# Where expert weights may land during the attention, and when the leftover pairs get their low part

## The chip, the core and the metric

The program runs on one NeuronCore of a Trainium2 chip. Its engines are PE (TensorE, matmuls; PEld is its weight load), DVE (VectorE), ACT (ScalarE), POOL (GpSimd) and SP (SyncE), which here issues nearly all DMA transfers. The metric is the device time of one execution in microseconds, as the median of several runs. Every DMA that SP issues goes into one queue, served by the core's 16 DMA engines.

## What is computed

Three layers follow one another, all in fp32 (as two fp32r parts, high and low, where PE takes fp32r):

```python
# attention, 8 batches x 8 heads x 576 positions x 64: decayed linear scores, no softmax
scores = q @ k.T / 8
ret = (scores * gamma[h] ** (i - j) * (i >= j)) @ v          # x: 4608 x 512
# soft mixture of 8 experts with 4 slots each
logits = x @ phi
slot_input = softmax(logits, axis=tokens).T @ x              # 32 x 512
slot_out[e] = relu(slot_input[e] @ w1[e]) @ w2[e]            # w1: 512x1024, w2: 1024x512
y = softmax(logits, axis=slots) @ slot_out                   # 4608 x 512
# bilinear layer
h = (y @ m1) * (y @ m2) @ w3
out = h @ w_out
```

y has only 32 rows of freedom per token, so the kernel never forms (y @ m1) * (y @ m2) per token. It forms products of pairs of slots once (ph, pl), multiplies them with W = w3 @ w_out into a matrix G, and multiplies each token's pairs of slot weights with G.

## The kernel before, in words

**Attention, 0 to about 160 us.** A loop over 36 units of 128 positions (`for u in range(NU)`, L758 on). Each unit issues, among others, the products of masked scores with v (`emit_pv`), the state update of the next unit (`emit_state(u + 1)`), the scores of unit u+2 (`emit_qk`), transposes (`emit_turns`) and the products with the state (`emit_inter`). Beside it the weights of the bilinear layer come in as 40 "pieces" of 512 KB (`load_piece`), each converted from 64-bit words by ACT, DVE and POOL (`conv_list`, one piece per unit, its last step on DVE is L497). A piece goes into one of four raw buffers and so waits until the piece four before it is converted. Pieces 30 to 39 are converted in the experts' stage.

**What sets the order of loads.** SP issues its list in order, and each transfer waits on SP until its target is free. Inside the loop loads are not written where they are decided: `later` puts a function into the list `waiting`, and `pace(behind)`, called at three points of each unit (behind `emit_pv`, behind `emit_qk`, and at the unit's end), takes one function from it and makes the loads that it issues wait for the PE instruction `behind`. A function may turn out to issue nothing: `load_k` past the last pair of blocks (it then only puts its buffer into `free`), or `load_expert` with no free place. In the last six units three `load_expert` are listed per unit.

**Places.** A place is a tile of 128 x 1024 fp32, 512 KB. qb (3), vb (3), rb (2) and kb (3) hold q, v, raw k and scaled k; kt_place holds turned k for the scores; p_places, s_place and xt_places hold masked scores, states and outputs. An expert's weights are eight loads of 512 KB, four for the first layer and four for the second, 64 in all; each takes the first tile in `free` (`load_expert`, L577 on). Places of q, v and raw k go into `free` in the loop after their last use; those of kb, kt_place, p_places and s_place behind the loop (L834).

**Experts' stage, about 169 to 250 us.** For each expert `emit_l1` (L600) and `emit_l2` (L620), between them the matmuls of W (`emit_Ws`, L564) and conversion steps. The four tiles of a layer go back into `free` as soon as it is issued, and further expert loads wait for them.

**G, about 256 to 290 us.** `pairs(cb)` forms the products of slot pairs of block cb on DVE (L1033 to L1035) and their high parts on ACT (L1036); `pairs_low(cb)` the low parts on DVE (L1040). `pleft` and `pleft2` are the leftover pairs, formed on POOL (L1053, L1056); L1061 (ACT) and L1062 (POOL) form their high and low part `phl`. `tick()` runs the eviction of the last W block (L572 on ACT, L573 on DVE). PE does twelve matmuls for each of eight blocks (`g_mm`, L1048), and behind block 0 sixteen for the leftover pairs (L1078), which read `phl` and all eight blocks of W. `pair_prep` (L642 to L649) prepares the tokens' pairs for the output stage on POOL and ACT during G.

**Output stage, about 290 to 400 us.** Nine tiles of 512 tokens, 52 matmuls each (L1114, L1123 to L1125), evicted and stored.

Of the kernel before, what the change touches and what calls it, by code (L numbers as in the profile page):

```python
# [16 lines left out]
ALU = mybir.AluOpType  # L17
# [4 lines left out]
NU = NTOK // 128  # L22
# [9 lines left out]
def retention_softmoe_bilinear(  # L32
# [257 lines left out]
    def emit_state(u):  # L290
        if tail(u):
            return
        x, c = units[u][1], block_of(u)
        for p in range(4):
            for h, a in halves:
                nc.tensor.matmul(  # L296
                    out=sbank[a, x, p], lhsT=k_tile(u)[:, x, p, h], rhs=v_tile(u)[:, 1 - h, x, p],
                    start=(c == 0 and x == 0 and p == 0), stop=True, skip_group_check=True,
                )
        if x == 1:  # L300
            Sn = sb[(c + 1) % 2]
            if c < 3:
                nc.scalar.copy(out=Sn, in_=sbank)
            else:
                for p in range(4):
                    nc.scalar.activation(out=Sn[:, :, p], in_=sbank[:, :, p], func=ACTF.Copy, scale=stab_sb[:, 8, p:p + 1])
# [105 lines left out]
    def after(i, j):  # L412
        tc.add_manual_dep(i.ins, j.ins.name, mybir.DependencyInfo(mybir.DependencyClass.Sync, mybir.DependencyReason.DATA), reason="pace")
# [173 lines left out]
    waiting = []  # L587

    def pace(behind):
        if waiting and behind is not None:  # L590
            for i in waiting.pop(0)():
                after(i, behind)

    hr_of, ht_of = {}, {}

# [57 lines left out]
    with tc.manual_schedule():  # L653
# [94 lines left out]
        for u in range(NU):  # L748
            T, r = divmod(u - 4, 4)

            def next_load():
                if nl[0] < min(len(pieces), done[0] + NRAW):
                    came.append(max(at[0], 2))
                    nl[0] += 1
                    return [load_piece(nl[0] - 1)]
                return load_expert()

            at[0], ended = u, None  # L758
            def next_k():
                if first_of_pair(u + 4):  # L760
                    scale_k(u + 4)
                    later(lambda n=pairs_in_order.index(units[u + 4][0]) + RBUF: load_k(n))

            if u > 0:
                next_k()
            run(subs)
            run_copies()
            run(adds)
            next_conv(u - 2)
            run_conv(1)  # L770
            if u == 2:
                emit_kt(5)
                misc[:] = [bank[2]]
            if u >= 6 and r == 2:
                emit_exp(T)
            done_pv = emit_pv(u)
            if u == 0:
                emit_kt(2)
            emit_xt(u)
            pace(done_pv)  # L780
            if u + 1 < NU:
                emit_state(u + 1)
            if u == 0:
                emit_kt(3)
                next_k()
                output_factors(2)
                output_factors(3)
            if u + 2 < NU:
                done_qk = emit_qk(u + 2)
                pace(done_qk)  # L790
                emit_p(u + 2)
            if u >= 8 and r == 0:
                emit_z(T - 1)
                emit_slots(T - 1)
            if u >= 2:
                ended = emit_turns(u - 4, u + 4)
            if u + 1 < NU:
                ended = emit_inter(u + 1) or ended
            if u == 1:
                emit_kt(4)  # L800
            if last_of_item(u):
                k = units[u][0]
                if k + VBUF < len(items):
                    later(lambda k=k: load_v(k + VBUF))
                else:
                    free.append(vb[k % VBUF])
            if u + 1 < NU and last_of_item(u + 1):
                k = units[u + 1][0]
                if k + QBUF < len(items):
                    later(lambda k=k: load_q(k + QBUF))  # L810
                else:
                    free.append(qb[k % QBUF])
            if u >= 7 and r == 3:
                emit_dT(T)
            run_conv(1)
            if u != 1:
                for _ in range(2 if u in TWICE else 1):
                    later(next_load)
            if u >= NU - 6:
                for _ in range(3):  # L820
                    later(load_expert)
            if u >= 2:
                pace(ended)
            if u >= 5 and r == 1:
                emit_logits(T)
            run_conv(4)
# [4 lines left out]
        run(subs)  # L831
        run_copies()
        run(adds)
        free.extend([*kb, *p_places, s_place, kt_place])  # L834
        load_expert(4)
        load_pieces()
        close_pool("psum")
# [218 lines left out]
        nc.gpsimd.tensor_tensor(out=twice, in0=half(0), in1=half(16), op=ALU.add)  # L1056
        pairs(0)
        pairs_low(0)
        tick()
        pairs(1)  # L1060
        nc.scalar.copy(out=phl[:, :, 0], in_=pleft2)  # L1061
        nc.gpsimd.tensor_tensor(out=phl[:, :, 1], in0=pleft2, in1=phl[:, :, 0], op=ALU.subtract)  # L1062
        which = [tmp.tile([32, 1], F32, tag=t, name=t) for t in ("beta", "negm")]
        for i in range(2):
            nc.vector.tensor_reduce(out=which[i], in_=ident[0:32, 16 * i:16 * i + 16], axis=AX.X, op=ALU.add)
# [141 lines left out]
```

## Time and profile before

| | |
|---|---|
| median of 3 runs | 400.6 us (399.61 to 401.44) |
| the profiled execution | 402.09 us |
| its span, first to last instruction | 400.3 us |
| PE busy | 378.1 us, 94% of the span |
| DVE, ACT, POOL busy | 254.7, 198.8, 172.7 us |
| moved by DMA | 108.75 MB, mean 272 GB/s |
| mean granted TensorE clock | 0.991 of full speed |

The span is cut into stages as above. The share of busy time is a mean over stages with different limits; within a stage one asks which wait ends last. PE's matmuls overlap, and their ends are modelled, so a busy PE need not be at its peak: start-to-start distances tell the rate. A granted clock of 1.00 is 2.4 GHz, one of 0.50 is 1.2 GHz.

### The profile page before, as it was taken

The numbers are of one execution on the slowest core, as the hardware profiler recorded it, in microseconds if no ns is written. First come the engines' busy times: TensorE is split into PE (matmuls) and PEld (weight loads), VectorE is DVE, ScalarE is ACT, GpSimd is POOL, SyncE is SP. The second block draws the span as 40 slices with busy tenths as digits, with TensorE's granted clock in tenths as the row PEclk, the third lists the DMA queues.
The fourth block names the chain that finished last, engine by engine and source line by source line (L and its number), as shares of the span: only waits on it lengthen the run. The fifth ranks groups of instructions, "written<-read, shape, count | busy, mean of one in ns | idle before, by whom it ended". The sixth has DMA issues, their size and how long they took to land.

```text
span 400.3 us, 10956 instructions
## 1 busy us (share of the span) xinstructions
PE 378.1 (94%) x4447; PEld 283.7 (71%) x4447; DVE 254.7 (64%) x432; ACT 198.8 (50%) x424; POOL 172.7 (43%) x158
## 2 busy tenths in 40 slices
PE   6989998989999998999999899979999999999995
PEld 4878787868978877655655444738787777787774
DVE  3648998998889996527775541468576353455400
ACT  2336686887778765235535321315434444443432
POOL 2633765666554464016544330116724335543420
PEclk9999999999999999999999999969999999999999
DMA  7899999999989987999999999690168989998643
GB/s 241 299 335 352 318 349 305 274 373 366 286 266 349 301 278 283 326 407 409 406 411 408 409 408 319 140 193 1 49 137 179 235 199 243 236 217 215 158 94 94
DMA packets 48211, 108.75 MB, mean 272 GB/s; under 512 B 7584, under 2 KB 10016, under 8 KB 48160
## 3 DMA queue, kind: packets, MB, share of 16 engines
q1 hardware_dynamic: 47008, 107.85, 84.0%
q8 instruction: 35, 0.57, 0.6%
q10 hardware_dynamic: 1152, 0.20, 0.3%
q14 instruction: 16, 0.13, 0.1%
HBM read 97.41 MB, written 10.62 MB: 270 GB/s over the span
## 4 chain that ended last, share of the span: by engine, by line
PE 70%; DMA 15%; DVE 8%; issue 3%; ACT 1%; POOL 1%; ACTq 0%; SPq 0%; POOLq 0%
PE bank L1123 9%; PE bank L1125 8%; PE bank L1124 8%; PE bank L564 7%; PE output L282 5%; PE scores L253 5%; DMA k<-in_ew 5%; PE bank L1048 5%; PE output L316 4%; DMA q<-in_ew 3%; DMA kt<-in_ew 3%; PE state L296 2%; PE bank L600 2%; PE bank L620 2%; DMA q<-in_q 2%
## 5 line engine op out<-in xcount | busy, mean ns | idle before, releaser
L644 POOL TENSOR_TENSOR cc<-mw_sb,cc 128x512 fp32r<-128x512 f32 x36 | 46.0, 1299 | 57.0 <-ACT cc L643 55.7
L564 PE MATMUL bank<-wop,w3p 128*128 128x512 f32 x192 | 50.8, 406 | 0.0
L523 POOL TENSOR_TENSOR vals<-vals,msb 128x512 int32<-128x512 int32 x24 | 30.9, 1288 | 41.4 <-DVE vals L497 34.6
L263 DVE TENSOR_TENSOR pm<-scores,msb 128x1024 f32<-128x1024 f32 x31 | 37.8, 1219 | 11.4 <-PE scores L253 11.1
L564 PEld LDWEIGHTS bank<-wop,w3p 128*128 128x128 f32 x192 | 34.1, 188 | 15.0 <-issue 8.7
L643 ACT CAST cc<-mw_sb 128x512 fp32r<-128x512 f32 x36 | 22.2, 616 | 44.0 <-DVE mw_sb L642 34.7
L1123 PE MATMUL bank<-w3p,cc 128*128 128x512 f32 x108 | 43.1, 399 | 0.0
L1125 PE MATMUL bank<-w3p,cc 128*128 128x512 f32 x108 | 42.1, 390 | 0.0
L1124 PE MATMUL bank<-w3p,cc 128*128 128x512 f32 x108 | 42.0, 389 | 0.0
L282 PE MATMUL output<-pm,v 128*64 128x128 f32 x512 | 35.6, 279 | 2.3 <-issue 1.8
L533 POOL TENSOR_TENSOR w3p<-vals,w3p 128x512 fp32r<-128x512 f32 x16 | 21.1, 1317 | 37.3 <-ACT w3p L528 33.9
L642 DVE TENSOR_TENSOR mw_sb<-lga,raw 128x512 f32<-128x512 f32 x32 | 29.2, 954 | 12.3 <-POOL cc L644 12.0
L253 PE MATMUL scores<-q,kt 64*128 64x128 f32 x496 | 36.0, 285 | 0.0
L523 POOL TENSOR_TENSOR mw_sb<-mw_sb,msb 128x512 int32<-128x512 int32 x16 | 20.5, 1281 | 30.6 <-DVE mw_sb L497 23.0
L1127 ACT ACTIVATE mw_sb<-bank,rz 128x512 f32<-128x512 f32 x36 | 24.7, 686 | 17.6 <-PE bank L1125 9.4
L282 PEld LDWEIGHTS output<-pm,v 128*64 128x64 f32 x512 | 27.5, 136 | 7.6 <-issue 5.9
L253 PEld LDWEIGHTS scores<-q,kt 64*128 64x128 f32 x496 | 30.1, 187 | 2.6 <-issue 0.8
L192 POOL TENSOR_TENSOR k<-kr,msb 128x512 f32<-128x512 f32 (+1 forms) x30 | 26.1, 890 | 5.4 <-DMA kr<-in_v 5.4
L504 ACT ACTIVATE msb<-raw 128x512 int32<-128x512 uint32 x40 | 27.8, 696 | 0.0
L220 ACT COPY kt<-pair 128x512 f32<-128x512 f32 x26 | 15.3, 587 | 25.0 <-PE pair L219 24.9
L1123 PEld LDWEIGHTS bank<-w3p,cc 128*128 128x128 f32 x108 | 20.3, 188 | 7.1 <-issue 2.9
L1125 PEld LDWEIGHTS bank<-w3p,cc 128*128 128x128 f32 x108 | 20.3, 188 | 4.4
(226 smaller groups left out, 767.2 us busy)
## 6 DMA issues: line engine op xcount, KB each, us to landing
q<-in_q SPq DMA_DIRECT2D x20, 512.0 KB, 6.2
raw<-expt SPq DMA_DIRECT2D x36, 256.0 KB, 4.5
kr<-in_v SPq DMA_DIRECT2D x16, 512.0 KB, 5.8
v<-in_v SPq DMA_DIRECT2D x16, 512.0 KB, 6.5
raw<-in_m SPq DMA_DIRECT2D x16, 512.0 KB, 6.1
raw<-in_w SPq DMA_DIRECT2D x16, 512.0 KB, 6.4
out_x<-mw_sb SPq DMA_DIRECT2D x64, 128.0 KB, 2.5
k<-in_ew SPq DMA_DIRECT2D x14, 512.0 KB, 10.2
```

What stands on the lines that cost most here:

```text
L192: (nc.vector if first else nc.gpsimd).tensor_tensor(out=Ks[:, :, 0:m, h], in0=K[:, 1 - h, :, 0:m], in1=ktab(c, h)[:, 0:m].unsqueeze(1).uns ...
L253: last = nc.tensor.matmul(out=ps[:, p], lhsT=ktb[u % 2][a, p], rhs=Q[a, :, x, p], start=True, stop=True)
L263: nc.vector.tensor_tensor(out=p_places[u % 2].rearrange("p (g t) -> p g t", g=8), in0=(pair if u == 1 else scores).rearrange("p (g t) -> p ...
L282: last = nc.tensor.matmul(out=xt_view(p)[side(p, h)], lhsT=v_tile(u)[:, 1 - h, x, p], rhs=p_main(u)[:, h, p], start=(block_of(u) == 0 and ...
L504: lambda: nc.scalar.activation(out=p.bitcast(I32), in_=lo, func=ACTF.Copy, scale=2.0 ** -29),
L523: nc.gpsimd.tensor_tensor(out=ti, in0=ti, in1=parts[i % 2].bitcast(I32), op=ALU.add)
L564: nc.tensor.matmul(out=ps, lhsT=x, rhs=y, start=(k8 == 0 and part == 0), stop=(k8 == 7 and part == 2))
L642: eng.tensor_tensor(out=e, in0=x, in1=y[:, m], op=ALU.mult)
L644: nc.gpsimd.tensor_tensor(out=cl[m], in0=e, in1=ch[m], op=ALU.subtract)
L1123: nc.tensor.matmul(out=ob, lhsT=ch[m][:, sl], rhs=gh[m], start=False, stop=False)
L1124: nc.tensor.matmul(out=ob, lhsT=ch[m][:, sl], rhs=gl[m], start=False, stop=False)
L1125: nc.tensor.matmul(out=ob, lhsT=cl[m][:, sl], rhs=gh[m], start=False, stop=(m == 3))
```

## The change

Four edits. `pace` takes functions from the list until one issues loads, so that a listed load without a place uses no pace point. The three places of scaled k go into `free` right behind the `emit_state` that reads them last, and kt_place behind the last `emit_qk` that reads it; in return they are no longer freed behind the loop. Three `load_expert` per unit are listed in the last nine units instead of six. And in G the two instructions for `phl` stand ahead of `tick()` and `pairs(1)`.

```diff
--- before.py
+++ after.py
@@ -587,9 +587,11 @@
     waiting = []
 
     def pace(behind):
-        if waiting and behind is not None:
-            for i in waiting.pop(0)():
-                after(i, behind)
+        loads = []
+        while waiting and not loads and behind is not None:
+            loads = waiting.pop(0)()
+        for i in loads:
+            after(i, behind)
 
     hr_of, ht_of = {}, {}
 
@@ -780,6 +782,9 @@
             pace(done_pv)
             if u + 1 < NU:
                 emit_state(u + 1)
+                n = pairs_in_order.index(units[u + 1][0]) if units[u + 1][1] else 0
+                if n + KBUF >= len(pairs_in_order):
+                    free.append(kb[n % KBUF])
             if u == 0:
                 emit_kt(3)
                 next_k()
@@ -789,6 +794,8 @@
                 done_qk = emit_qk(u + 2)
                 pace(done_qk)
                 emit_p(u + 2)
+                if u + 2 == NU - 2:
+                    free.append(kt_place)
             if u >= 8 and r == 0:
                 emit_z(T - 1)
                 emit_slots(T - 1)
@@ -816,7 +823,7 @@
             if u != 1:
                 for _ in range(2 if u in TWICE else 1):
                     later(next_load)
-            if u >= NU - 6:
+            if u >= NU - 9:
                 for _ in range(3):
                     later(load_expert)
             if u >= 2:
@@ -831,7 +838,7 @@
         run(subs)
         run_copies()
         run(adds)
-        free.extend([*kb, *p_places, s_place, kt_place])
+        free.extend([*p_places, s_place])
         load_expert(4)
         load_pieces()
         close_pool("psum")
@@ -1056,10 +1063,10 @@
         nc.gpsimd.tensor_tensor(out=twice, in0=half(0), in1=half(16), op=ALU.add)
         pairs(0)
         pairs_low(0)
+        nc.scalar.copy(out=phl[:, :, 0], in_=pleft2)
+        nc.gpsimd.tensor_tensor(out=phl[:, :, 1], in0=pleft2, in1=phl[:, :, 0], op=ALU.subtract)
         tick()
         pairs(1)
-        nc.scalar.copy(out=phl[:, :, 0], in_=pleft2)
-        nc.gpsimd.tensor_tensor(out=phl[:, :, 1], in0=pleft2, in1=phl[:, :, 0], op=ALU.subtract)
         which = [tmp.tile([32, 1], F32, tag=t, name=t) for t in ("beta", "negm")]
         for i in range(2):
             nc.vector.tensor_reduce(out=which[i], in_=ident[0:32, 16 * i:16 * i + 16], axis=AX.X, op=ALU.add)
```

Lines behind the edits shift: L600 becomes L602, L620 L622, L1036 L1043, L1048 L1055, L1061 L1066, L1062 L1067, L1078 L1085.

How the order moves, first on SP in units 28 to 33 of the attention, before; `raw` is a piece, a load from `in_ew` an expert load, the number behind a name tells tiles of one kind apart (kr_104 and kr_105 are raw k, k_106 to k_108 scaled k).

```order
L183 DMA v_101<-in_v 128x2x512
L479 DMA raw<-in_w 128x512
L176 DMA q_99<-in_q 128x1024
L479 DMA raw<-in_w 128x512
L184 DMA v_102<-in_v 64x512 x2
L479 DMA raw<-in_w 128x512
L583 DMA kr_104<-in_ew 128x1024
L583 DMA kr_105<-in_ew 128x1024
L583 DMA q_100<-in_ew 128x1024
L479 DMA raw<-in_w 128x512
L583 DMA v_103<-in_ew 128x1024
L479 DMA raw<-in_w 128x512
```

All expert loads of the loop but the very first (ew0) stand behind the last load of v (L184).

The same stretch of SP's list after the change.

```order
L583 DMA kr_104<-in_ew 128x1024
L183 DMA v_101<-in_v 128x2x512
L479 DMA raw<-in_w 128x512
L583 DMA k_107<-in_ew 128x1024
L176 DMA q_99<-in_q 128x1024
L479 DMA raw<-in_w 128x512
L583 DMA kr_105<-in_ew 128x1024
L184 DMA v_102<-in_v 64x512 x2
L479 DMA raw<-in_w 128x512
L583 DMA k_108<-in_ew 128x1024
L583 DMA q_100<-in_ew 128x1024
L479 DMA raw<-in_w 128x512
```

Three expert loads now stand among the last loads of v and q, the second of them in a place of scaled k; the pieces and loads of q and v keep their order.

SP's list from there to the first load into a place of masked scores (pm_94), which is behind the loop, before.

```order
L583 DMA q_98<-in_ew 128x1024
L583 DMA v_101<-in_ew 128x1024
L583 DMA q_99<-in_ew 128x1024
L479 DMA raw<-in_w 128x512
L583 DMA v_102<-in_ew 128x1024
L583 DMA k_106<-in_ew 128x1024
L583 DMA k_107<-in_ew 128x1024
L583 DMA k_108<-in_ew 128x1024
L583 DMA pm_94<-in_ew 128x1024
```

The three places of scaled k are loaded last of these, behind the loop.

The same after the change.

```order
L583 DMA kt<-in_ew 128x1024
L583 DMA v_103<-in_ew 128x1024
L583 DMA k_106<-in_ew 128x1024
L583 DMA q_98<-in_ew 128x1024
L479 DMA raw<-in_w 128x512
L583 DMA v_101<-in_ew 128x1024
L583 DMA q_99<-in_ew 128x1024
L583 DMA v_102<-in_ew 128x1024
L479 DMA raw<-in_w 128x512
L583 DMA pm_94<-in_ew 128x1024
```

From the first to pm_94 there are 12 expert loads now, where there were 11, and the four into k places and kt stand inside the loop; up to v_102, the last place freed in the loop, 12 are issued instead of 8 (one more, ew0, much earlier in both).

ACT at the start of G, before; the copies into `wop` are the high parts of pairs, L572 is the eviction of the last W block, the load into `gs` is L1061.

```order
L1036 CAST wop<-mw_sb 128x128 x2
L1036 CAST wop<-mw_sb 128x256
L572 CAST w_3532<-bank_2622 128x512
L1036 CAST wop<-bank_2622 128x512
L1061 CAST gs<-mw_sb 128x8x32
L1036 CAST wop<-bank_2627 128x512
L1085 COPY acc<-bank_2626 32x512
L1036 CAST wop<-bank_2622 128x512
L647 CAST cs<-mw_sb 128x512
```

L1061 stands behind the eviction and behind the high part of block 1.

ACT at the start of G after the change.

```order
L1043 CAST wop<-mw_sb 128x128 x2
L1043 CAST wop<-mw_sb 128x256
L1066 CAST gs<-mw_sb 128x8x32
L572 CAST w_3534<-bank_2625 128x512
L1043 CAST wop<-bank_2625 128x512
L1043 CAST wop<-bank_2630 128x512
L1092 COPY acc<-bank_2629 32x512
L1043 CAST wop<-bank_2625 128x512
L649 CAST cs<-mw_sb 128x512
```

The copy into `gs` has moved up by two rows, ahead of the eviction; POOL's row for L1062 keeps its place between L1056 and the tokens' first pairs.

## Rows read from the trace of the kernel before

**Rows 1.** The page: busy time by engine; shares of the chain that ended last.

```profile
PE 378.1 (94%) x4447; PEld 283.7 (71%) x4447; DVE 254.7 (64%) x432; ACT 198.8 (50%) x424; POOL 172.7 (43%) x158
...
PE 70%; DMA 15%; DVE 8%; issue 3%; ACT 1%; POOL 1%; ACTq 0%; SPq 0%; POOLq 0%
```

**Rows 2.** Windows: length, busy us (count) by engine, clock, DMA share, GB/s.

```profile
136.00:160.00 24.00, 22.61 (x528) 18.70 (x528) 19.85 (x34) 16.11 (x38) 11.63 (x10) 1.00 0.82 275
175.00:240.00 65.00, 61.80 (x459) 34.54 (x458) 38.59 (x90) 27.43 (x60) 28.87 (x22) 1.00 1.03 409
200.00:250.00 50.00, 45.95 (x332) 24.29 (x322) 24.84 (x57) 16.44 (x37) 16.75 (x13) 1.00 1.02 392
264.00:270.00 6.00, 6.00 (x14) 3.18 (x15) 3.24 (x6) 0.59 (x1) 1.20 (x1) 0.50 1.01 191
```

**Rows 3.** Chain of waits, 236 to 292 us: start, length, what held it.

```profile
239.26 8.99 DMA k<-in_ew
...
264.00 6.64 PE bank L1078 x16
270.63 19.06 PE bank L1048 x84
```

**Rows 4.** Timeline of PE, experts 1 and 5: start, length, line, operation.

```profile
179.43 0.64 PE L600 MATMUL bank<-v,slotm 128*32 128x256 f32 x8
...
181.30 3.06 PE L564 MATMUL bank<-wop,w3p 128*128 128x512 f32 x12
...
219.14 1.07 PE L600 MATMUL bank<-k,slotm 128*32 128x256 f32 x16
...
223.36 2.34 PE L564 MATMUL bank<-wop,w3p 128*128 128x512 f32 x9
```

**Rows 5.** Timelines of SP and DVE; then single issues at 153.9, 156.4, 178.4 us (KB, us to landing).

```profile
182.42 0.33 SPq L479 DMA_DIRECT2D raw<-in_w  x1
...
181.66 0.69 DVE L497 SCALAR_TENSOR_TENSOR vals<-raw,vals 128x512 uint32<-128x512 uint32 x1
...
raw<-in_w SPq DMA_DIRECT2D x1, 512.0 KB, 3.8
...
q<-in_ew SPq DMA_DIRECT2D x1, 512.0 KB, 4.1
...
q<-in_ew SPq DMA_DIRECT2D x1, 512.0 KB, 10.2
```

**Rows 6.** The issue at 140.11 us (KB, us to landing), and ACT's first read of it.

```profile
raw<-in_w SPq DMA_DIRECT2D x1, 512.0 KB, 5.3
...
150.91 0.70 ACT L502 ACTIVATE vals<-raw 128x512 f32<-128x512 f32 x1
```

**Rows 7.** Timelines of PE, ACT, POOL and DVE where G begins.

```profile
258.24 2.94 PE L1048 MATMUL bank<-w,wop 128*128 128x512 f32 x12
...
258.62 0.41 ACT L1036 CAST wop<-mw_sb 128x256 fp32r<-128x256 f32 x1 [0.82 <-DVE mw_sb L1035]
...
262.73 0.41 ACT L1061 CAST gs<-mw_sb 128x256 fp32r<-128x256 f32 x1
...
257.39 0.75 POOL L1056 TENSOR_TENSOR mw_sb<-mw_sb 128x256 f32<-128x256 f32 x1
263.22 0.72 POOL L1062 TENSOR_TENSOR gs<-mw_sb,gs 128x256 fp32r<-128x256 f32 x1 [5.08 <-ACT gs L1061]
...
259.67 0.68 DVE L573 TENSOR_TENSOR w<-bank,w 128x512 fp32r<-128x512 f32 x1
```

**Rows 8.** Timelines of ACT, DVE and PE, inside G and at its end.

```profile
271.76 0.62 ACT L647 CAST cs<-mw_sb 128x512 fp32r<-128x512 f32 x1
...
266.01 0.67 DVE L1035 TENSOR_TENSOR bank<-bank,mw_sb 128x480 f32<-128x480 f32 x1
...
289.40 1.89 DVE L1097 TENSOR_TENSOR w3p<-bank,w3p 128x512 fp32r<-128x512 f32 x3 [3.97 <-POOL cc L644]
...
290.90 0.40 PE L1124 MATMUL bank<-w3p,cc 128*128 128x512 f32 x1
```

## The prediction

> **What bounds the kernel now.** I read the page first: PE is busy for 378.1 of 400.3 us, and the chain that ended last is PE for 70% and DMA for 15% [rows 1]. So PE sets the time, and what can be won is where PE waits or runs slowly. The windows show two such places [rows 2]. From 200 to 250 us PE is busy for 45.95 of 50.00 us, while the DMA moves 409 GB/s at a share of 1.03 over 175 to 240 us: the experts' weights come no faster. From 264 to 270 us the granted clock is 0.50, which is the 1.2 GHz level. Between 136 and 160 us, by contrast, the DMA moves 275 GB/s and has room.
>
> The chain of waits names the links [rows 3]. The experts' stage ends with the landing of the last load, issued at 239.26 and 8.99 us on its way, at 248.25. In G the sixteen matmuls L1078 start at 264.00 and take 6.64 us, after which 84 matmuls take 19.06 us, 0.227 each. PE's work before them ended at 261.18 (258.24 and 2.94 us), and what they wait for is POOL's low part of the leftover pairs, L1062, itself 5.08 us idle for ACT's L1061 [rows 7]. And 6.64/16 is 0.415 us per matmul where the next ones take 0.227: the wait cost time twice, once as a wait and once as a lower clock.
>
> How much of the experts' stage is waiting? With nothing missing, one expert's first layer runs from 179.43 to the next group at 181.30, 1.87 us. Expert 5's runs from 219.14 to 223.36, 4.22 us [rows 4]: this layer alone loses 2.35 us. The idle that the window 200 to 250 shows is 4.05 us, and durations of matmuls are modelled, so somewhat more may hide in them. PE can win 4.05 us there at least, if the loads come in time.
>
> **Part 1, the loads (pace, the places of k, 3 x 3 units more).** No bytes and no instructions are added: 64 expert loads stay 64. They only start earlier. In the order on SP, 8 expert loads stand ahead of the point where the attention loop has drained before the change, and 12 after it; every later load keeps its position relative to the computation. So the queue is 4 loads ahead. The price of one, with the queue full, is 512 KB at 409 GB/s, 1.28 us [rows 2]. Four are 5.1 us. The room is there: 409 less 275 GB/s over 24 us are 3.2 MB, and four loads are 2.1 MB.
>
> What gives some of it back: SP works its list in order, and piece 34 of the bilinear weights reuses a buffer that DVE has to read first. That read ends at 182.35 (181.66 and 0.69) and SP issues the piece at 182.42 [rows 5]. This hangs on experts 0 and 1, which wait for no load, so it does not move. The load ahead of it in the list, issued at 178.42, landed 10.2 us later, at 188.6; four loads sooner that is 183.5. A load on an empty queue takes 3.8 to 4.1 us to land [rows 5], so the piece lands at 186.2 to 186.5, where right behind its forerunner it would have landed at 184.8. The queue runs dry for 1.4 to 1.7 us; I take 1.5. The same wait of pieces 35 to 39 costs nothing, for the loads behind piece 34 have free places by then and fill the queue again. So the last load lands 5.1 less 1.5, or 3.6 us sooner, and the stage ends as much sooner, since 3.6 is less than the 4.05 that PE can win. Bounds: 0 to 5.1, the lower if the room before 160 us is not used, the upper if the queue never runs dry.
>
> The Trainium skill ("DMA: Bandwidth & Descriptors", section "Anatomy of one DMA — SWDGE (gpsimd) path") fits a lone transfer by 2.0 us plus bytes over 436 GB/s, which for 512 KB is an estimate of 3.2 us. The rows have 3.8 and 4.1 us on SP's queue, so I keep the rows; by the page the dry stretch would be about 0.9 us and the sum 0.6 us better.
>
> What the earlier loads could harm is the attention, whose own loads share the queue. Piece 29, issued at 140.11, lands 5.3 us later, at 145.4, and ACT first reads it at 150.91 [rows 6]: 5.5 us of slack, while at most two expert loads (2.6 us) stand newly ahead of any such load. The loads of q and v are listed four or five units ahead of their use. SP's new waits are for the PE instructions that last read the k places, and these come before the pace point that the load waits for anyway. I cost this at nothing; without the slack it would cost up to 1.3 us for each expert load ahead.
>
> **Part 2, the leftover pairs.** ACT's copy L1061 and POOL's L1062 stand before the change behind the next block's pairs: L1061 ran at 262.73, L1062 at 263.22 [rows 7]. Their input was ready when POOL's L1056 ended at 258.14. After the change L1061 follows ACT's third copy L1036 (258.62 and 0.41), so it ends at about 259.4 and L1062 (0.72) at about 260.2, 1.0 us before PE has finished the twelve matmuls L1048 at 261.18. L1061 now stands ahead of ACT's copy L572 of the last W block and delays it, and with it DVE's low part (L573, 259.67 to 260.35), by at most 0.41 us; only the sixteenth matmul reads that. So the sixteen start at 261.2, with no pause that could lower the clock (it is 1.00 from 200 to 250 us with 4.05 us of short pauses) [rows 2]: PE goes from 261.18 through them in 16 times 0.227, 3.6 us, and not in 9.45 (270.63 less 261.18). That is 5.8 us.
>
> What is late next: the pair work for the output stage, on POOL and ACT. ACT's L647 ran at 271.76, held by the copy that waits for L1078. After the change it is held by ACT's copy of the fourth pairs, for which DVE's L1035 ends at 266.68 (266.01 and 0.67); with that copy's 0.6 us L647 starts at 267.4, 4.4 us sooner and not 5.8 [rows 8]. So this chain falls 1.4 us back against PE. At its end DVE's first L1097 (289.40, 1.89 us for three) ends at 290.0 and PE needs it at 290.90: slack 0.9. 1.4 less 0.9 are 0.5 us of waiting. Part 2 gives 5.8 less 0.5, or 5.3 us. Bounds: 2.8 (the wait alone, clock low anyway) to 5.8.
>
> **Sum.** 3.6 and 5.3 are 8.9 us of the span of 400.3. The profiled execution took 402.09 us, 1.5 above the median of 400.6; what lies around the span is not touched. 400.6 less 8.9 is **391.7 us**.
>
> **The rivals.** First, *the queue stays full and the chain of pairs keeps up*: 5.1 and 5.8, 10.9 us, **389.7**. For it: 10.2 us from issue to landing, that is eight loads queued [rows 5]. Against it: the piece at 182.42, the 1.4 us that the pair work falls back, and that of the 5.1 us only 4.05 are seen as idle of PE.
>
> Second, *the loads ahead are given back*: the experts' places come free only as PE reads them, and SP stops at every piece, so the advance melts before expert 4 and only 0 to 1.5 us remain: with 5.3 that is **393.8 to 395.3**. For it: the list is in order and one stop of 1.5 us is already in my sum. Against it: in the window 175 to 240 us the queue never went short, at a share of 1.03 [rows 2].
>
> Third, *the clock falls all the same*: if L1062 came later than 261.2, or PE paused elsewhere in that stretch, the sixteen would still take 6.64 us; only 2.8 us are won, with 3.6 that is **394.2**. Against it: 1.0 us of margin.
>
> Fourth, *slower*: the expert loads pushed into the attention make its last pieces late. Of those behind an expert load only pieces 28 and 29 are read inside the loop, each by ACT and DVE in a unit of its own, and DVE's mask products, which PE needs, stand behind. It decides when a piece takes more than 5.3 and 5.5, 10.8 us to land; the kernel is slower than 400.6 only if the two together cost over 8.9 us, 4.5 each, that is landings of 15.3 us: **401 and more**. Landings of 10.2 us are seen only with a full queue, which the room of 3.2 MB speaks against.
>
> That the change does not do what it says is out: the order of SP and ACT shows both moves.
>
> **How the numbers follow.** Forecast 0.63 (its own range 390.3 to 393.4), first rival 0.12, second 0.13, third 0.09, fourth 0.03. The range from 389.4 to 395.2 holds all but the fourth rival and an edge of the second. A measurement here tells 0.5%, 2.0 us, from no change: faster 0.95, same 0.03, slower 0.02.
>
> **What would show it.** In the profile after: DMA well above 275 GB/s from 136 to 160 us; the last expert load landing near 244.6; a short dip of the DMA near 184 us; PE idle from 200 us to the stage's end much under 4 us; L1062 ending before the twelve L1048 do, no idle before L1078, granted clock 1.00 through G and the sixteen in 3.6 us; then a wait of about half a microsecond of the first L1124 (its new line) for DVE's L1097. The prediction is wrong if units of the attention get longer, if the last load still lands after 247, or if G starts with the clock at 0.50.

## The result, and the profile after

The changed kernel takes 396.1 us (median of 5, 395.4 to 398.3) where before takes 400.2 (median of 5): a ratio of 0.989 (95%: 0.986 to 0.992), 4.1 us. On two later chips the ratio was 0.990 (0.987 to 0.994) and 0.986 (0.981 to 0.990). The forecast was 391.7, with a range from 389.4 to 395.2: the sign was right, the gain less than half of the 8.9 us forecast, and the time just outside the range. The profiled execution took 397.17 us, its span 395.4.

Windows of the changed kernel, columns as in [rows 2]; the last is new (before had a share of 1.03 and 409 GB/s in it).

```profile
136.00:160.00 24.00, 22.71 (x521) 19.01 (x521) 19.89 (x34) 16.39 (x38) 11.39 (x9) 1.00 0.98 341
175.00:240.00 65.00, 63.38 (x470) 36.61 (x469) 39.47 (x91) 27.42 (x60) 29.79 (x23) 1.00 0.98 382
200.00:250.00 50.00, 46.86 (x351) 25.12 (x350) 26.04 (x62) 16.79 (x39) 17.75 (x14) 1.00 1.02 393
264.00:270.00 6.00, 6.00 (x28) 4.82 (x27) 5.93 (x11) 3.62 (x6) 2.44 (x3) 1.00 0.95 184
175.00:200.00 25.00, 25.00 (x181) 14.71 (x180) 14.62 (x32) 12.24 (x26) 12.04 (x10) 1.00 0.91 339
```

Two signs of the forecast are there: the DMA is full from 136 to 160 us (0.98, was 0.82), and G runs at a clock of 1.00 (was 0.50). But right behind the attention the DMA now falls short, 339 GB/s where it moved 409. What was carried early is missing there.

SP's timeline shows why: start, length on the queue, line, target and count.

```profile
164.27 2.56 SPq L583 DMA_DIRECT2D xts<-in_ew  x3
172.84 0.33 SPq L583 DMA_DIRECT2D k<-in_ew  x1
173.28 0.37 SPq L583 DMA_DIRECT2D kr<-in_ew  x1
178.62 0.33 SPq L583 DMA_DIRECT2D q<-in_ew  x1
179.44 0.60 SPq L583 DMA_DIRECT2D kt<-in_ew  x1
180.13 0.38 SPq L583 DMA_DIRECT2D v<-in_ew  x1
184.11 0.33 SPq L479 DMA_DIRECT2D raw<-in_w  x1
184.53 0.38 SPq L583 DMA_DIRECT2D k<-in_ew  x1
```

Three single issues of it, at 166.50, 184.11 and 184.53 us (KB, us to landing).

```profile
xts<-in_ew SPq DMA_DIRECT2D x1, 512.0 KB, 10.7
...
raw<-in_w SPq DMA_DIRECT2D x1, 512.0 KB, 3.7
...
k<-in_ew SPq DMA_DIRECT2D x1, 512.0 KB, 6.1
```

The 19th expert load, the last with a place at once, lands at 177.18 us; in before it landed at 182.16. The lead is there, 5.0 us. Then SP issues nothing from 166.50 to 172.84: every place is full until expert 0's first layer has read its tiles. Two loads go, then it stops again until the second layer at 178.6, and again until 184.1, there for piece 34's buffer. From 177.18 to the 30th load at 199.06 thirteen transfers land in 21.88 us, where the full queue's 1.28 each make 16.6: 5.2 us are lost. In before the same thirteen take 17.56 us, up to 199.72, so that 4.3 of the 5.0 us of lead are gone by the 30th load. From there the queue is full in both kernels, and the last load lands where it did.

Chain of waits and PE's timeline of the changed kernel: the last load, landing at 248.40 (248.25 in [rows 3]), and the rows that answer to [rows 3] and [rows 8]. The last row is of before.

```profile
238.56 9.84 DMA v<-in_ew
...
258.41 2.94 PE L1055 MATMUL bank<-w,wop 128*128 128x512 f32 x12
261.19 3.84 PE L1085 MATMUL bank<-w,gs 128*64 128x512 f32 x16
...
285.95 0.50 PE L1130 MATMUL bank<-w3p,cc 128*128 128x512 f32 x1
...
290.57 0.50 PE L1123 MATMUL bank<-w3p,cc 128*128 128x512 f32 x1
```

In G the sixteen (now L1085) start without a wait and take 3.84 us, not 6.64. From the first twelve to the first output matmul L1130 there are 27.54 us, where the trace of before has 32.33 (258.24 to 290.57, its first L1123): 4.8 us less.

One thing came that was not forecast. PE stops in the middle of the scores' matmuls of unit 25, for nothing that the profile shows, and expert 0 starts at 171.28 us, where the trace of before has 169.62. The first two rows are of the changed kernel, the last is of before.

```profile
125.49 0.27 PE L253 MATMUL scores<-q,kt 64*128 64x128 f32 x1 [1.19 <-issue]
...
171.28 0.64 PE L602 MATMUL bank<-ew,slotm 128*32 128x256 f32 x8
...
169.62 0.64 PE L600 MATMUL bank<-ew,slotm 128*32 128x256 f32 x8
```

### The profile page after: what moved, and what is told of

The parts are those of the page before. It is cut to its first block, busy times and chain, and to the rows that moved or that the text cites. A ratio compares the mean times of both kernels' runs of the same rounds, so it can differ in the third digit from the quotient of the medians.

```text
span 395.4 us, 10962 instructions
## 1 busy us (share of the span) xinstructions
PE 377.4 (95%) x4447; PEld 284.3 (72%) x4447; DVE 254.5 (64%) x432; ACT 198.8 (50%) x424; POOL 172.5 (44%) x158
## 4 chain that ended last, share of the span: by engine, by line
PE 72%; DMA 13%; DVE 11%; ACT 1%; issue 1%; SPq 0%; ACTq 0%; DVEq 0%
PE bank L1130 9%; PE bank L1132 8%; PE bank L1131 8%; PE scores L253 7%; PE output L282 7%; PE bank L564 7%; DMA v<-in_ew 5%; PE output L316 4%; PE state L296 3%; DMA q<-in_ew 3%; DMA st<-in_ew 3%; PE bank L622 2%; PE bank L602 2%; PE pair L215 2%; DMA v<-in_v 2%; PE bank L1121 2%
## 5 line engine op out<-in xcount | busy, mean ns | idle before, releaser
L1130 PE MATMUL bank<-w3p,cc 128*128 128x512 f32 x108 | 43.1, 399 | 0.0
L253 PE MATMUL scores<-q,kt 64*128 64x128 f32 x496 | 37.3, 290 | 1.2 <-issue 1.2
L533 POOL TENSOR_TENSOR w3p<-vals,w3p 128x512 fp32r<-128x512 f32 x16 | 21.1, 1317 | 35.0 <-ACT w3p L528 32.3
L253 PEld LDWEIGHTS scores<-q,kt 64*128 64x128 f32 x496 | 31.1, 192 | 4.2 <-issue 2.4
L1130 PEld LDWEIGHTS bank<-w3p,cc 128*128 128x128 f32 x108 | 20.3, 188 | 7.1 <-issue 2.9
```

Of the source, the lines that this page charges most:

```text
L253: last = nc.tensor.matmul(out=ps[:, p], lhsT=ktb[u % 2][a, p], rhs=Q[a, :, x, p], start=True, stop=True)
L1130: nc.tensor.matmul(out=ob, lhsT=ch[m][:, sl], rhs=gh[m], start=False, stop=False)
```

## The experiments

**Each part alone, twice.** `phl_only` is before with the last edit; `loads_only` is the changed kernel with those two lines back in their old place.

```diff
         pairs_low(0)
-        nc.scalar.copy(out=phl[:, :, 0], in_=pleft2)
-        nc.gpsimd.tensor_tensor(out=phl[:, :, 1], in0=pleft2, in1=phl[:, :, 0], op=ALU.subtract)
         tick()
         pairs(1)
+        nc.scalar.copy(out=phl[:, :, 0], in_=pleft2)
+        nc.gpsimd.tensor_tensor(out=phl[:, :, 1], in0=pleft2, in1=phl[:, :, 0], op=ALU.subtract)
```

> The kernel before with the last edit alone: the two instructions for phl stand ahead of tick and pairs(1). The traces of before and after put what G gains at 4.8 us (from the end of the last expert's second layer to the first L1130: 41.30 us before, 36.52 after). Theory A, the earlier loads are worth nothing: this kernel gains what the whole change gained, 4.1 to 4.8 us, and lies at 395.4 to 396.1 us. Theory B, the earlier loads lose something, because they lengthen the attention (its end is 1.67 us later in the trace of after): this kernel beats the whole change by 1 us or more, 394.0 to 395.1 us. Theory C, the prediction's: the loads are worth 3.6 us and the phl edit less than it seems: 399 us or more.

> The changed kernel with the two instructions for phl back behind tick and pairs(1): only the loads are taken ahead. Theory A, what was taken ahead is given back where the experts hold all places: within 0.7 us of the kernel before, last expert load landing within 0.5 us of the 248.25 us of before, a DMA share near 0.91 from 175 to 200 us as in the trace of after (1.03 before). Theory B, the loads lengthen the attention: 0.5 to 1.7 us slower than before, the first layer of expert 0 starting near 171.3 us (169.6 before). Theory C, the prediction's: 3.6 us faster, last landing near 244.6 us.

> loads_only again, beside the next two on one chip. Its time was 1.8 us below before (0.3 to 3.3), yet its trace shows no earlier end of the experts' stage. Theory A, the edits on the loads are worth nothing: within 0.7 us of before. Theory B, they are worth about 1.8 us, which single traces do not resolve: 1 to 2.5 us faster than before.

> phl_only again on the chip of the other two. Theory A, the phl edit brings the whole 4.1 us: 3.5 us or more faster than before, within 0.7 us of after_3. Theory B, it brings the wait alone in most runs (2.06 us by the second trace of before, where the clock stayed at 1.00) and the clock's part in some: 2 to 3 us faster than before, and 1 to 2 us slower than after_3.

> The changed kernel a third time, as the measure for the other two: 4 us faster than before by all theories. By theory A phl_only_2 equals it and loads_only_2 equals before; by theory B its gain is the sum of theirs, 1.8 and 2.2 us. In its trace the pause near 125 us in the scores' matmuls is there again, with 0.9 to 3 us.

Measured as ratios to before: phl_only 0.994 (0.991 to 0.997) and 0.989 (0.986 to 0.993), or 2.2 and 4.4 us; loads_only 0.996 (0.992 to 0.999) and 0.993 (0.990 to 0.996), or 1.8 and 2.7 us; after_3 0.986. So neither "all of it is phl" nor "the loads lose" holds. Both parts gain, phl about 3.3 us and the loads about 2.3 as the means of two, with intervals of over 1 us either side.

The time of the last landing shows none of the loads' gain: 249.21 and 248.26 us in the two traces of loads_only, against 248.13 and 249.12 in those of phl_only. But the experts start later in loads_only. Expert 0's first matmuls and the last load, first of phl_only, then of loads_only:

```profile
169.98 0.64 PE L600 MATMUL bank<-ew,slotm 128*32 128x256 f32 x8
239.09 9.04 DMA k<-in_ew
```

```profile
172.82 0.64 PE L602 MATMUL bank<-ew,slotm 128*32 128x256 f32 x8
240.15 9.06 DMA v<-in_ew
```

Counted from expert 0's start, the last load lands after 76.39 and 76.53 us in loads_only, and after 77.12, 75.71 and 75.96 in the three traces of the changed kernel. In before, before_2 and the two of phl_only it lands after 78.63, 77.79, 78.15 and 79.41. So the earlier loads shorten the stage by some 2 us; what hides it is the start of expert 0, at 169.6 to 170.0 us in those four traces and at 171.3 to 175.7 in these five.

Some 0.6 us of the gain lies behind the stage: from the first twelve matmuls of G to the end, loads_only takes 140.42 us, before 142.10, and 1.17 of the difference is the sixteen (5.47 against 6.64), so 0.5 is left; against before_2 (below) the same sum gives 0.6. The other 1.7 of the 2.3 us fit a stage that is some 2 us shorter and an attention that gives part of it back. How much it gives back in a median run single traces do not resolve, since the attention's end moves by more than that from one execution to the next.

**Before once more, for G.**

> The kernel before once more, for a second trace of it. What the phl edit can save depends on what the late phl costs: in the first trace the sixteen matmuls L1078 wait 2.8 us and then take 6.64 us at a granted clock of 0.50 to 0.59, and that run was 1.5 us above the median of before. In loads_only, with the same late phl, they took 5.47 us at a clock of 0.82. Theory A, the clock's part of the loss differs from run to run and the first trace had a large one: here the sixteen take 4 to 6 us, and the distance from the end of the last expert's second layer to the second group L1114 is 50 to 51.5 us, not 52.35. Theory B, the loss is the same in every run: 6.6 us and 52.3 us. Both: no pause of 0.9 us or more in the scores' matmuls near 125 us.

PE's timelines of before_2 and then of loads_only, both with the late phl, and the window 262 to 268 us of each.

```profile
257.36 2.93 PE L1048 MATMUL bank<-w,wop 128*128 128x512 f32 x12
263.11 3.90 PE L1078 MATMUL bank<-w,gs 128*64 128x512 f32 x16 [2.81 <-POOL gs L1062]
...
286.95 0.50 PE L1123 MATMUL bank<-w3p,cc 128*128 128x512 f32 x1
262.00:268.00 6.00, 4.89 (x22) 3.22 (x23) 4.66 (x9) 1.77 (x4) 1.98 (x2) 1.00 1.08 205
```

```profile
264.94 5.47 PE L1085 MATMUL bank<-w,gs 128*64 128x512 f32 x16 [2.81 <-POOL gs L1069]
262.00:268.00 6.00, 3.19 (x10) 1.73 (x10) 5.90 (x12) 1.48 (x3) 1.99 (x2) 0.82 1.08 215
```

The wait of 2.81 us is the same, the price is not. In before_2 the clock stays at 1.00 and the sixteen take 3.90 us; in loads_only it falls in part and they take 5.47. Of five traces with the late phl (before, loads_only, loads_only_2, before_2, pace_only) the sixteen took 6.64, 5.47, 5.48, 3.90 and 3.90. Theory A holds, though 3.90 lies just below the 4 to 6 that it gave. From the twelve to the first output matmul before_2 needs 29.59 us, so against the changed kernel's 27.54 phl saves 2.05 us where the clock holds and 4.8 where it falls as in the first trace; against the 27.90 us of phl_only, without the earlier loads, it is 1.7 and 4.4. The mean of the clock's part over the five traces, (6.64 + 5.47 + 5.48 + 2 x 3.90)/5 less 3.90, is 1.2 us: with it phl is worth 2.9 to 3.2 us, near the 3.3 of the two timings.

**Does the lead die for want of places?** In the experts' stage six places are set aside for blocks of W, one behind each second layer from expert 0 on. They can be set aside two experts later and still be in time.

```diff
-                    if len(wplaces) < 8:
+                    if e >= 2 and len(wplaces) < 8:
                         wplaces.append(free.pop(0))
```

> The changed kernel, with each of the six places that the experts' stage sets aside for blocks of W taken from the free ones two experts later than now (from expert 2 on and not from expert 0 on; the third block is evicted during expert 2). So two more places stand open to expert loads from expert 0's second layer on. Theory A, in 172 to 200 us the loads wait for places: two loads of 1.28 us more are queued there, the DMA's share from 175 to 200 us rises above the 0.91 of after, the last load lands 1 to 2.6 us sooner and the time falls by as much, to 393.5 to 395.1 us. Rival, the time is set by the rate of the full queue from 200 us on and by PE's own work: the dry places move but the last load lands within 0.5 us of the 248.4 of after, 395.6 to 396.6 us.

> The changed kernel itself, once more, on the same chip and in the same rounds as the next three. All theories: 4 us faster than before. What it tells: whether the pause of PE at 125.5 us (1.19 us in the middle of the scores' matmuls L253, with nothing that the profile shows as its cause, and not in the traces of before and of phl_only) is there again. If it belongs to the earlier loads, it is there with 1.0 to 2.0 us, and the experts' first layer starts at 170.2 us or later; if it is chance, it is gone, and the layer starts at 169.6 to 170.0 us as in before and phl_only.

> The changed kernel with the places for W's blocks set aside two experts later, the same file as w_places_late, now beside the changed kernel on one chip. Theory A (the lead of the loads is lost for want of places): 2 to 3 us faster than after_2, last landing at 245 to 246 us, as in the first trace (245.55; 248.40 in after). Rival (the first trace was a good one): within 0.7 us of after_2.

> The kernel before with the phl edit and with W's places set aside two experts later, but without the loads taken ahead. Theory A, lead and places need each other: in before the queue was never short (share 1.03 from 175 to 240 us), so more places have nothing to carry; the last load lands at 247.5 to 248.5 us, and the time is that of phl_only, 397.6 to 398.3 us, 2 us or more above w_places_2. Rival, the places alone bring the gain, and the edits on the loads nothing at all: last landing near 245.5 us, time within 0.7 us of w_places_2.

On one chip: after_2 396.5 us, w_places_2 394.4 (ratio to before 0.983, 0.981 to 0.986), phl_w_places 397.4 (0.991, 0.989 to 0.993). In the first timing, on another chip, w_places_late had 0.990 (0.984 to 0.995), with runs from 393.9 to 399.1. The last load lands at 247.75, 245.70 and 248.22 us; w_places_late had 245.55. But expert 0 started at 172.04 us in after_2, and at 169.78 and 170.24 in the two traces with more places, which the edit doesn't explain. Counted from there the last load lands after 75.93 and 75.31 us with more places, and after 77.12, 75.71 and 75.96 in the changed kernel. So two more places brought the kernel whose loads are ahead 2 us in the one timing that had the changed kernel beside it; its traces show 0.6 us of that in the stage, as means, and the earlier timing is no better than the changed kernel's own 0.989. The clock has a part in that: its three runs with a mean granted clock of 0.998 or more took 393.9 to 395.5 us, the other three 397.1 to 399.1. To the kernel whose loads are not ahead the places bring nothing: it lies where phl_only lies. That the lead lacks places agrees with all of this, but this experiment alone does not show it; the next two bear on it as well.

**The same bytes taken away early and late.** Four expert loads are shortened to an eighth; most of these four tiles of weights is left out.

```diff
+            cols = 128 if 18 <= len(ew) - 1 < 22 else 1024   # short_late: 48 to 51
-            loads.append(nc.sync.dma_start(out=ew[-1], in_=(ew1, ew2)[j // 4][e][:, 1024 * (j % 4):1024 * (j % 4) + 1024]))
+            loads.append(nc.sync.dma_start(out=ew[-1][:, 0:cols], in_=(ew1, ew2)[j // 4][e][:, 1024 * (j % 4):1024 * (j % 4) + cols]))
```

> The changed kernel with four expert loads (the 19th to the 22nd, issued between 166 and 179 us) shortened from 512 to 64 KB each, so most of these four tiles of expert 2's weights is left out; the places, the order and all waits stay. The DMA has 3.5 loads' worth less to move, 4.5 us at 1.28 us each. Theory A, the loads wait for places there and the DMA is dry at this point anyway: it is only dry for longer, the last load lands less than 1.5 us sooner than at 248.4. Rival, the stage's end follows from the sum of bytes after the attention: the last load lands about 4.5 us sooner, near 244, and the stage ends 3 to 4 us sooner.

> The changed kernel with four later expert loads (the 49th to the 52nd, the first layer of expert 6, issued between 217 and 222 us) shortened from 512 to 64 KB each, so most of these four tiles is left out; places, order and waits stay. The same 3.5 loads' worth, 4.5 us, are taken away as in short_early, where they moved the last landing by 0.8 us. Theory A, places bind early and the full queue binds late: here the last load lands 3 to 4.5 us sooner than the 247.75 to 248.40 of the changed kernel, at 243.5 to 245.4 us. Rival, places or PE bind throughout: it moves by less than 1.5 us, as in short_early.

short_early's last load lands at 247.63 us, 0.8 before that of the changed kernel's first trace and 0.1 before that of its second; from the 18th load, the last full one ahead of the short ones, to the 36th it needs 32.8 us, the changed kernel 33.4 and 32.3. Taking 4.5 us of transfers out at that point bought next to nothing. In short_late the attention ended 3.7 us late (expert 0 at 174.96 us): behind a pause of PE of 3.06 us the granted clock was 0.50 from 125.9 to 132.7 us. So I compare within its own stage: from the 36th load to the last it needs 34.4 us, the changed kernel 39.1 and 38.4 in two traces. That is 4.0 to 4.7 us, about all of the 4.5 that were taken out. Early in the stage places bind, late the full queue does.

**PE frees the places sooner.** With the same number of W's matmuls, but fewer between the first experts:

```diff
-                emit_Ws(max(0, min(55, 4 + (4 * e + t + 1) * 52 // 28) - nW[0]))
+                emit_Ws(max(0, min(55, 4 + int(52 * ((4 * e + t + 1) / 28) ** 1.3 + 0.001)) - nW[0]))
```

> w_places_2, and the matmuls of W shifted towards the later experts (the share of 52 due by step s of 28 is (s/28) to the power 1.3 in place of s/28: 3 and not 5 groups of three behind the first layer of expert 0, the same sum at the end). The experts then free their places sooner at the beginning, where the trace of w_places_late still has four gaps between landings of 2.08, 2.59, 1.69 and 2.19 us, 3.4 us above the full queue's 1.28 each. Theory A, places bind until the queue is full for good: most of these gaps close, the last load lands 1.5 to 3.4 us sooner; PE has only 1.75 us of idle left from 200 to 246 us, so the time falls by 0.5 to 2 us against w_places_2. Rival, PE is the limit by now or the later W blocks make PE late: the same time or up to 1.5 us slower.

392.7 us, a ratio of 0.980 (0.978 to 0.983): 1.7 us below w_places_2 and 3.8 below after_2 on the same chip, and the best of the study. First windows of w_places_2, then of w_later.

```profile
175.00:200.00 25.00, 25.00 (x196) 14.32 (x198) 14.97 (x36) 12.58 (x27) 12.11 (x9) 1.00 0.95 361
200.00:246.00 46.00, 44.29 (x327) 23.99 (x321) 24.71 (x57) 16.08 (x36) 16.71 (x13) 1.00 1.02 398
```

```profile
175.00:200.00 25.00, 24.20 (x198) 13.61 (x191) 14.08 (x37) 10.75 (x24) 7.68 (x7) 1.00 1.02 392
200.00:244.00 44.00, 43.96 (x322) 25.83 (x322) 25.18 (x56) 18.08 (x39) 20.54 (x16) 1.00 1.02 399
```

Behind expert 0's second layer SP went on at 177.04 us in w_places_2 and goes on at 175.43 in w_later; the DMA's share from 175 to 200 us is back at 1.02, and the last load lands at 243.85, which is 73.64 us behind expert 0's start, 2.3 less than in w_places_2. From 200 us on PE is busy for 43.96 of 44.00 us: both limits are met at once, and the chain of waits shows the last load ending with PE's last but one piece of work.

```profile
239.75 2.26 PE bank L564 x9
242.01 1.84 PE bank L622 x12
243.85 0.04 issue
243.90 1.05 PE bank L622 x4
```

**The edits on the loads, one by one.**

> The kernel before with the first edit alone (pace takes functions from the list until one issues loads); places, listed units and phl as before. It tells where the pause of PE near 125 us comes from: all seven traces with the edits on the loads have it (0.93 to 2.01 us in the middle of L253), the three without them do not. Theory A, it comes with pace, which changes which PE instruction each load waits for from the first units on: the pause is here too, 0.9 to 2 us. Theory B, it comes with the expert loads that stand among those of q and v from unit 27 on: it is not here. The last expert load lands at 247.5 to 249 us by both, since no place is free earlier.

> The changed kernel with the three expert loads listed in the last six units again and not in nine; pace, the early places of k and kt, and phl stay. Still 12 loads stand ahead of the places of masked scores in the list, but they begin behind the attention's last load of v. Theory A, what is taken ahead is lost later anyway: the 19th load lands 2 us or more later than in after (177.18 to 178.34), and the last load still lands at 247.5 to 248.5. Theory B, the nine units matter: the last load lands 1 us or more later than that. On the pause near 125 us: it has been in all eight traces with all three edits on the loads and in none of the six without one of them; if it needs the nine units, it is gone here.

> w_later with pace as in the kernel before, so that listed functions that issue nothing use up a pace point again; places of k freed early, nine units, W's places late, W's matmuls late and phl early stay. Theory A (pace brings the pause near 125 us): the pause is gone, the experts begin 1 to 1.5 us sooner, and 12 loads are still ahead of the masked scores' places, so the time is 0.5 to 1.5 us below w_later: 391.2 to 392.2 us at before's 400.4 to 401.0, a ratio of 0.976 to 0.979. Theory B (the pause comes with the expert loads): the pause stays, and the time is that of w_later or up to 1 us more, a ratio of 0.980 to 0.983.

pace_only (one run, 400.0 us) pauses for 0.7 us near 125 us, between what the two theories say, and its last load lands at 248.82. six_units (one run, 396.2 us) has a pause of 1.46 us; its 19th load lands at 181.36, with hardly any lead, and its last at 247.08, 76.17 us behind expert 0's start, as in the changed kernel. So the three more units move the loads and not the end of the stage. old_pace is slow, 0.992 (0.989 to 0.995) where w_later has 0.980, and not for the reason that I gave: there is no pause, but this time the list of loads is jammed. SP's timeline of old_pace:

```profile
141.48 0.33 SPq L479 DMA_DIRECT2D raw<-in_w  x1
147.67 0.33 SPq L176 DMA_DIRECT2D q<-in_q  x1
...
155.05 1.16 SPq L184 DMA_DIRECT2D v<-in_v  x2
156.37 0.46 SPq L479 DMA_DIRECT2D raw<-in_w  x1
```

With three expert loads listed per unit and three pace points, functions that issue nothing push the rest back: the last load of v goes out at 155.05 us (143.04 in the changed kernel), the 19th expert load lands at 185.20 and the last at 251.22. Part of that is a late start: in this trace the granted clock falls to 0.50 twice in the attention, at 91.2 and 162.8 us, and expert 0 starts at 173.81. Counted from there the two land after 11.40 and 77.41 us, in w_later after 6.90 and 73.64. With nine units listed, `pace` has to skip empty functions.

The pause of PE in the scores' matmuls is 0.9 to 3.1 us in all eleven traces that have both the new pace and the early places. In the seven others there is none in five, 0.5 us in before_2 and 0.7 in pace_only. So its size goes with the program, not with chance alone. The first expert load that the edits move goes out at 132 us, after it, so it isn't their traffic. The DMA packets in the traces point to instructions: in the eighteen traces PE has 44 pauses of over 0.5 us for which the profile names no cause, and each ends 1.26 to 1.62 us behind the landing of a 16 KB packet on the queue q8, which the profile calls an instruction queue and which has 35 such packets in an execution. Pauses at random would lie so close behind a packet in fewer than one case of ten. Why the packet comes late at this place with these edits stays open.

## Why the prediction failed

**What bounds the kernel**: right. The last landing ends the experts' stage in both kernels, and G lost a wait and a lower clock.

**Part 1, forecast 3.6 us; measured 1.8 and 2.7 alone. The stage is some 2 us shorter, counted from expert 0's start, and by the last landing it ends no sooner.** The step that failed is "every later load keeps its position relative to the computation. So the queue is 4 loads ahead". Room on the DMA and 5.1 us of lead were right: 5.0 us at the 19th load. But a load further back needs a place that an expert frees at a fixed time, and can't move ahead of that. The trace of before held the answer: its 20th expert load went out at 172.95 us, and the first places it can use come free when expert 0's first layer ends, near 171.5 (169.62 and 1.87). A lead of more than 1.5 us had nowhere to go. That is about what the stage got: the 20th load goes out 3.33 us behind expert 0's start in before and 1.56 behind it in the changed kernel, 1.8 us sooner. I looked at one stop, piece 34, and costed it at 1.4 to 1.7 us; it came much as I wrote (issued at 184.11, 1.7 us later than in before, as expert 0 was, and landed 3.7 us behind that), but the stops for places at 166.50 to 172.84 and 173.28 to 178.62 came ahead of it. Against the second rival, "the loads ahead are given back", I set the share of 1.03 in before; that share says that a queue without a lead never ran short, and nothing of one that is ahead. The mechanism of this rival is what happened; I had given it 0.13, at 0 to 1.5 us in the stage.

Behind a nearly empty queue the rows' 3.8 to 4.1 us held (3.7 and 4.0 here, the piece at 184.11 and the load at 178.62). The prediction called that queue empty, but in all four cases the load ahead had not landed yet. The estimate of 3.2 us for a lone transfer from the Trainium skill ("DMA: Bandwidth & Descriptors", section "Anatomy of one DMA — SWDGE (gpsimd) path"), which is for GpSimd's path, lies below all four; no run here shows a lone transfer on SP's queue.

**Part 2, forecast 5.3 us; measured 2.2 and 4.4 alone, 4.8 between the traces of before and after.** The mechanism came as described: L1066 at 259.11 us, L1067 done before PE needed it, no wait, clock 1.00, sixteen in 3.84 us (forecast 3.6). Behind it 0.7 us came back, where the forecast had 0.5: PE waits 0.5 us for DVE's low part of G's last pairs (L1055 behind L1047), and from the first L1121 to the first L1130 it needs 1.16 us (0.94 in before). The term that was mis-sized is the clock's 3.0 us: I took one execution's price for every run's, and over the five traces with the late phl it is 1.2 us in the mean, from 0 to 2.7. The hint stood in my own sum: the profiled execution was 1.5 us above the median, and I took the clock's loss out of the median all the same. The second trace bears it out: that execution is 3.5 us shorter (398.55 us, not 402.09), and 2.7 of these lie between the first twelve and the first output matmul.

The Trainium skill ("TensorE: Matmul & The Clock Gate", section "What's actually happening") says that the window in which the gate looks at PE runs freely and is not set back when a kernel starts. If so, it is chance where in it a pause falls. The traces fit that, though they do not prove it: one wait of 2.81 to 2.83 us, five times, with the sixteen behind it at 6.64, 5.47, 5.48, 3.90 and 3.90 us.

**The attention**: costed at nothing, and this, too, was wrong. PE's pause near 125 us, which the trace of before does not have at that place, took 0.9 us or more in every trace of the full change, and expert 0 started 1.7 us later in the first of them, which is about what the stage gained. The pieces weren't late, so the fourth rival didn't come.

**Sum.** About 2.3 for the loads and 3.3 for phl, by their own timings, against 3.6 and 5.3; together that is more than the 4.1 of the change itself, within the intervals. With the places that the lead needs, and W's matmuls out of the way, the kernel reaches 392.7 us, 1.0 above the forecast; the forecast for the change as it was left that condition out.

## What to carry to other kernels

A transfer that is issued sooner ends a stage sooner only if all that follow it can move too: for each load behind it, ask what frees its target and when, and compare that time with its issue in the trace; the smallest slack is what a lead is worth. A share of the DMA at 1.0 says that the queue was never short at its present lead, not that it would take a larger one. And where the profiled execution is above the median, ask first whether the loss to be removed is that excess, above all if it is the clock's, and take a second trace before costing it.

## What was not expected of the hardware

- The clock's answer to one and the same wait differs: after 2.81 us of waiting the granted clock in the window 262 to 268 us was 0.59 (before, first trace), 0.82 (loads_only) and 1.00 (before_2).
- A queue that had run short did not go on at its full rate at once: of two loads issued 0.42 us apart at 184.11 and 184.53 us, the second landed 2.84 us behind the first (187.80 and 190.64), where the full queue lands one each 1.28 us. It is not always as much: of two issued at 144.22 and 144.66 us in before, the second landed 1.64 us behind the first (148.00 and 149.64).
- PE paused for 0.9 to 3.1 us at one place in unit 25, with no wait that the profile shows, in every trace of a program with the new pace and the early places; in the seven traces of other programs it paused there for 0 to 0.7 us. All these pauses end 1.26 to 1.62 us behind the landing of a 16 KB packet of an instruction queue.
